# x enters SBUF through DMA transposes from DRAM instead of plain loads, TensorE transposes and PSUM copies (gated mix of a linear-attention block and a one-token mixture, one Trainium2 core)

## The chip, the cores and the metric

The kernel runs on one core of one Trainium2 chip. The metric is the device time of one execution in microseconds (us); a smaller number is better. Times below are either the measured time of whole executions or come from one profiled execution of the kernel.

## The reference, cut to what matters

The input x has 2048 rows (tokens) of 1024 numbers in bf16. Branch A is a linear attention with 32 heads of 32, whose feature map is a pair of softmaxes; branch B passes x through and adds a gated feed-forward result to the one row with the largest logit. A sigmoid gate mixes the two.

```
x = A_x
g = _sigmoid((x * gate_w).sum(-1, keepdims=True))
...
q, k, v = qkv[0], qkv[1], qkv[2]            # qkv from x @ wqkv
pk = jnp.einsum("bhsd,hdf->bhsf", k, w_phi)
phi_k = jnp.concatenate([_softmax(pk, axis=-1), _softmax(-pk, axis=-1)], axis=-1)
kv = jnp.einsum("bhsf,bhsd->bhfd", phi_k, v)
...
r = x @ w_r
idx = jnp.argsort(-r, axis=-1)[:, :C]       # C = 1: one row is chosen
...
return g * a + (1 - g) * b
```

## The kernel before

The work is cut into 16 token tiles of 128 rows (t = 0 to 15), and most stages into 32 units u = 2t + half, a unit being one token tile and 16 heads. Every product with x on TensorE needs x with its columns on the partitions, so the kernel builds `xT`, 128 partitions x 8 blocks x 2048 tokens in bf16, once and keeps it. How `xT` is filled is what the change touches.

**x.** `xload(t)` (L109 to L112) loads one tile of 128 x 1024 from DRAM on the SP queue into a pool of four buffers (`xs`). `xT_tile(t)` (L122 to L134) does eight 128 x 128 transposes on TensorE into a PSUM tile `pT` (L128), copies it into `xT` on VectorE for even t (L130) and on ScalarE for odd t (L132), and then issues the load of tile t + 4.

**Weights.** `wv_sb` (two loads of 1 MB), `wk_raw` (2 MB), later `wo_sb` and `wq_raw` (2 MB each) and 21 chunks of 1 MB of the feed-forward weights also go through the SP queue. `prep_j` (L136 to L147) folds `w_phi` into the k weights, for one block j of eight: eight TensorE transposes of `wk_raw` into PSUM (`pTw`, L139), a VectorE copy `wT` (L141), eight matmuls with the block-diagonal `BDm` into two PSUM tiles (`pW`, L146), and two ScalarE copies into `wkf` (L147). `pTw` and both `pW` share the two buffers of the pool `psB`. The first k unit needs all eight blocks of `wkf`. The q weights go through `prep_j` later.

**Logits and route.** `logits_and_route` (L149 on) multiplies all 16 tiles of `xT` with two columns (L155, 8 matmuls a tile, results in `small_ps`), makes the gates from one column, and finds the row with the largest logit from the other: the column is transposed, moved into one row `r_row` by a small DMA on SP (L168), and searched on VectorE (MAX8, L170; FIND_INDEX8, L172). The index picks a column `xsT` of `xT` (L175), which the feed-forward chunks (L202) then use.

**k units, q units, tail.** A k unit is 8 matmuls for v (L292), 8 for k (L304), a softmax pair over VectorE (mx L243, mn L244, d L251, ssum L263, rs L267), POOL (d L247, phi L269) and ScalarE (pks L235, e L256 and L257), and 8 matmuls that add to `kv_b` (L323). q units (L352 on) and the output projection (L428) follow.

The order of the calls is written by hand in an event list with keys, but the framework's scheduler then decides the order in which instructions stand on each engine; each engine runs its list in order. A wait of an instruction holds up everything behind it on its engine. DMAs use eight completion semaphores in turn, so a DMA on SP waits at least for the one eight places earlier to land.

The calls ahead of the k units are:

```
    for t in range(4):
        xT_tile(t)
    for u in sorted(v_startup, key=lambda u: (u % 2, u)):
        k_v(u)
    for j in range(KB):
        prep_j(wk_raw, wkf, j)
        if j % 2 == 1:
            xT_tile(4 + j // 2)
    for t in range(8, NT):
        xT_tile(t)
```

`v_startup` holds five units. In the program before, TensorE's list starts with transposes of tiles 0 to 2, then v units mixed with tile 3, then `prep_j` blocks mixed with the transposes of later tiles and with the logits of the tiles that are already there; the logits of tiles 13 to 15 and all of the routing stand among the first k units.

Of the kernel before, what the change touches and what calls it, by code (L numbers as in the profile page):

```python
# [8 lines left out]
BF = mybir.dt.bfloat16  # L9
# [8 lines left out]
P = 128  # L18
# [4 lines left out]
NT = S // P  # L23
KB = D // P
# [13 lines left out]
def kernel(  # L38
# [4 lines left out]
    nc = tc.nc  # L43
    x2 = A_x.rearrange("b s d -> (b s) d")
# [8 lines left out]
    psA = ctx.enter_context(tc.tile_pool(name="psA", bufs=2, space=PSUM))  # L53
# [10 lines left out]
    ident = const.tile([P, P], BF, name="ident")  # L64
# [17 lines left out]
    xT = big.tile([P, KB, S], BF, name="xT")  # L82
# [24 lines left out]
    xtiles = {}  # L107

    def xload(t):  # L109
        xt_ = xs.tile([P, D], BF, name="xs_t", tag="xs")  # L110
        nc.sync.dma_start(out=xt_[:], in_=x2[t * P:(t + 1) * P, :])
        xtiles[t] = xt_  # L112

    xload(0)
    nc.sync.dma_start(out=wv_sb[:, :, 0:512], in_=w_v[:, :, 2 * D:2 * D + 512])
    for t in range(1, 4):
        xload(t)
    nc.sync.dma_start(out=wv_sb[:, :, 512:D], in_=w_v[:, :, 2 * D + 512:3 * D])
    wk_raw = raw.tile([P, KB, D], BF, name="wk_raw", tag="wraw")
    nc.sync.dma_start(out=wk_raw[:], in_=w_v[:, :, D:2 * D])  # L120

    def xT_tile(t):  # L122
        if t not in xtiles:
            xload(t)
        xt_ = xtiles.pop(t)
        pT = psA.tile([P, KB, P], BF, name="pT", tag="pA")
        for kb in range(KB):
            nc.tensor.transpose(out=pT[:, kb, :], in_=xt_[:, kb * P:(kb + 1) * P], identity=ident[:])  # L128
        if t % 2 == 0:
            nc.vector.tensor_copy(out=xT[:, :, t * P:(t + 1) * P], in_=pT[:])  # L130
        else:
            nc.scalar.copy(out=xT[:, :, t * P:(t + 1) * P], in_=pT[:])  # L132
        if t + 4 < NT:
            xload(t + 4)  # L134

    def prep_j(w_raw, wf, j):  # L136
        pT = psB.tile([P, KB, P], BF, name="pTw", tag="pB")
# [354 lines left out]
# [10 lines that stand above are left out]
# [43 lines left out]
```

## Time and profile before

| what | value |
|---|---|
| time, median of 2 executions | 356.94 us (355.91 and 357.97) |
| span of the profiled execution | 356.3 us |
| busy: TensorE, VectorE, ScalarE, POOL | 318.7, 258.5, 211.8, 202.8 us |
| L128, transposes of x on TensorE | 128 instructions, 3.8 to 39.4 us |
| L130 / L132, copies of `pT` | 8 of 0.68 us on VectorE / 8 of 1.02 us on ScalarE |
| first k matmul (L304) | 39.4 us |
| last copy of `wkf` (L147) ends | 41.7 us |
| loads of x tiles (`xs_t`) | 16 of 256 KB, 5.5 us to landing (median) |
| DMA bytes in the execution | 43.6 MB |

The span is the time from the first to the last instruction of one execution. "Busy" of TensorE counts modelled ends of pipelined matmuls, so a busy TensorE is not TensorE at its peak. PE is TensorE, PEld its weight loads, DVE VectorE, ACT ScalarE, SP the queue that issues most DMAs.

### The profile page before, as it was taken

How to read it: one execution, taken by the hardware profiler on the slowest of the kernel's cores; microseconds unless marked ns; L12 is line 12 of the kernel's file. 1: busy time of each engine (PE TensorE's matmuls, PEld its weight loads, DVE VectorE, ACT ScalarE, POOL GpSimd, SP SyncE). 2: the span in 40 equal slices, each digit the busy share in tenths (PEclk: the TensorE clock that was granted, in tenths of full speed). 3: DMA queues.
4: the chain of work that ended last, by engine and by line, in shares of the span. 5: the costliest groups of instructions: out<-in, count | busy, mean ns of one | idle time of the engine just before them, and what ended most of it. 6: DMA issues, size and time to landing. Idle time of an engine off the chain costs nothing. (4 is left out here: it accounts for less than half of the span.)

```text
span 356.3 us, 8221 instructions
## 1 busy us (share of the span) xinstructions
PE 318.7 (89%) x3322; PEld 189.1 (53%) x3372; DVE 258.5 (73%) x455; ACT 211.8 (59%) x333; POOL 202.8 (57%) x231
## 2 busy tenths in 40 slices
PE   2998996989989899698989898999999999999982
PEld 1578552445555555354446475555555555556640
DVE  3034288877987975688887989888888888887641
ACT  1456645535556655254554679777777777778630
POOL 1000056467776763577778978687777766665101
PEclk9999999989999999999999999999999999999998
DMA  8997920028823033333336660012221111122111
GB/s 253 375 386 238 324 87 2 0 87 272 261 94 118 2 120 118 120 118 120 120 118 237 233 245 31 31 59 61 61 60 61 60 60 46 59 61 62 47 59 30
DMA packets 33894, 43.60 MB, mean 122 GB/s; under 512 B 2624, under 2 KB 23104, under 8 KB 33856
## 3 DMA queue, kind: packets, MB, share of 16 engines
q1 hardware_dynamic: 32704, 43.00, 35.5%
q8 instruction: 26, 0.43, 0.5%
q10 hardware_dynamic: 1120, 0.07, 0.2%
q14 instruction: 12, 0.10, 0.1%
q0 software_dynamic: 32, 0.00, 0.0%
HBM read 38.87 MB, written 4.20 MB: 121 GB/s over the span
## 5 line engine op out<-in xcount | busy, mean ns | idle before, releaser
L247 POOL TENSOR_TENSOR d<-pks,mx 128x512 bf16<-128x512 bf16 x64 | 67.1, 1049 | 89.1 <-DVE mx L243 82.4
L263 DVE TENSOR_REDUCE ssum<-e 128x32 f32<-128x1024 bf16 x64 | 77.4, 1211 | 33.3 <-ACT e L257 33.2
L256 ACT ACTIVATE e<-d 128x512 bf16<-128x512 bf16 x64 | 40.5, 633 | 61.7 <-POOL d L247 55.4
L269 POOL TENSOR_TENSOR phi<-e,rs 128x1024 bf16<-128x1024 bf16 x32 | 61.2, 1912 | 22.0 <-DVE rs L267 21.0
L304 PE MATMUL pk<-wkf,xT 128*128 128x512 bf16 x242 | 61.7, 385 | 4.6 <-DVE d L251 4.1
L352 PE MATMUL pq<-wqf,xT 128*128 128x512 bf16 x237 | 59.2, 379 | 3.9 <-ACT pks L235 2.0
L292 PE MATMUL pv<-wv_sb,xT 128*128 128x512 bf16 x248 | 61.1, 385 | 0.8 <-issue 0.2
L428 PE MATMUL kv_b<-wo_sb,oT 128*128 128x512 bf16 x247 | 57.1, 379 | 1.5 <-ACT oT L416 1.0
L243 DVE TENSOR_REDUCE mx<-pks 128x16 f32<-128x512 bf16 x64 | 42.4, 662 | 17.2 <-ACT pks L235 13.9
L257 ACT ACTIVATE e<-d 128x512 bf16<-128x512 bf16 x64 | 40.4, 631 | 7.6 <-POOL d L249 7.2
L374 ACT COPY eT<-eT_ps 128x1024 bf16<-128x1024 bf16 x32 | 32.6, 1019 | 17.6 <-PE eT_ps L370 17.6
L244 DVE TENSOR_REDUCE mn<-pks 128x16 f32<-128x512 bf16 x64 | 42.8, 669 | 0.0
L428 PEld LDWEIGHTS <-oT 128*128 128x128 bf16 x256 | 24.8, 98 | 30.2 <-ACT oT L416 1.1
L304 PEld LDWEIGHTS <-xT 128*128 128x128 bf16 x256 | 24.2, 98 | 30.2 <-issue 5.9
L292 PEld LDWEIGHTS <-xT 128*128 128x128 bf16 x256 | 24.1, 99 | 27.3 <-issue 3.1
L352 PEld LDWEIGHTS <-xT 128*128 128x128 bf16 x256 | 24.1, 97 | 27.0 <-issue 2.7
L277 POOL TENSOR_TENSOR e<-e,rho 128x512 bf16<-128x512 bf16 x32 | 33.6, 1051 | 2.5
L249 POOL TENSOR_TENSOR d<-pks,mn 128x512 bf16<-128x512 bf16 x32 | 33.6, 1049 | 1.4
L431 DVE SCALAR_TENSOR_TENSOR o_out<-kv_b,gate,xg 128x512 bf16<-128x512 f32 x32 | 23.8, 744 | 10.6 <-PE kv_b L428 7.9
L141 DVE COPY wT<-pTw 128x1024 bf16<-128x1024 bf16 x16 | 10.9, 683 | 19.7 <-PE pTw L139 19.7
L296 ACT CAST vaug<-pv 128x512 bf16<-128x512 f32 x32 | 18.6, 581 | 8.5 <-PE pv L292 8.4
L235 ACT CAST pks<-pk 128x512 bf16<-128x512 f32 x32 | 18.5, 578 | 5.7 <-PE pk L304 4.7
(94 smaller groups left out, 432.9 us busy)
## 6 DMA issues: line engine op xcount, KB each, us to landing
wch<-in_B_w_gate_dram SPq DMA_DIRECT2D x7, 1024.0 KB, 6.0
wch<-in_B_w_up_dram SPq DMA_DIRECT2D x7, 1024.0 KB, 5.1
wchd<-in_B_w_down_dram SPq DMA_DIRECT2D x7, 1024.0 KB, 5.2
xs_t<-in_A_x_dram SPq DMA_DIRECT2D x16, 256.0 KB, 5.5
xin<-in_A_x_dram SPq DMA_DIRECT2D x16, 256.0 KB, 2.7
out_dram<-o_out SPq DMA_DIRECT2D x32, 128.0 KB, 1.7
wv_sb<-in_A_wqkv_dram SPq DMA_DIRECT2D x2, 1024.0 KB, 5.7
wk_raw<-in_A_wqkv_dram SPq DMA_DIRECT2D x1, 2048.0 KB, 10.1
```

Source lines behind the costliest of these rows:

```text
L243: nc.vector.tensor_reduce(out=mx[:], in_=st["ps"][:], axis=AX.X, op=ALU.max)
L244: nc.vector.tensor_reduce(out=mn[:], in_=st["ps"][:], axis=AX.X, op=ALU.min)
L247: nc.gpsimd.tensor_tensor(out=d1[:], in0=st["ps"][:], in1=_bc(mx[:], [P, HH, DH]), op=ALU.subtract)
L249: nc.gpsimd.tensor_tensor(out=d2[:], in0=st["ps"][:], in1=_bc(mn[:], [P, HH, DH]), op=ALU.subtract)
L256: nc.scalar.activation(out=e[:, :, 0, :], in_=st["d1"][:], func=ACTF.Exp)
L257: nc.scalar.activation(out=e[:, :, 1, :], in_=st["d2"][:], func=ACTF.Exp, scale=-1.0)
L263: nc.vector.tensor_reduce(out=ssum[:].rearrange("p h s -> p (h s)"), in_=e[:].rearrange("p h s f -> p (h s) f"), axis=AX.X, op=ALU.add)
L269: nc.gpsimd.tensor_tensor(out=phi[:].rearrange("p h s f -> p (h s) f"), in0=e[:].rearrange("p h s f -> p (h s) f"), in1=_bc(rs[:].rearrang ...
L292: nc.tensor.matmul(pvf, lhsT=xT[:, kb, t * P:(t + 1) * P], rhs=wv_sb[:, kb, hf * 512:(hf + 1) * 512], start=(kb == 0), stop=(kb == KB - 1))
L304: nc.tensor.matmul(pkf, lhsT=xT[:, kb, t * P:(t + 1) * P], rhs=wkf[:, kb, hf * 512:(hf + 1) * 512], start=(kb == 0), stop=(kb == KB - 1))
L352: nc.tensor.matmul(pqf, lhsT=xT[:, kb, t * P:(t + 1) * P], rhs=wqf[:, kb, hf * 512:(hf + 1) * 512], start=(kb == 0), stop=(kb == KB - 1))
L428: nc.tensor.matmul(kv_b[nh][:], lhsT=oT[:, kb, :], rhs=wo_sb[:, kb, sl], start=(kb == 0), stop=(kb == KB - 1))
```

## The change

`xT_tile(t)` becomes one DMA on the SP queue that reads 128 rows of x from DRAM and writes them transposed into `xT`. The first four loads of x that stood among the weight loads are gone, so `wv_sb` and `wk_raw` are now issued ahead of all of x. The 128 transposes of x on TensorE, the 16 copies out of PSUM, and the 16 plain loads are no longer there; `prep_j`, the logits and everything later are unchanged in the source.

```
-    xload(0)
     nc.sync.dma_start(out=wv_sb[:, :, 0:512], in_=w_v[:, :, 2 * D:2 * D + 512])
-    for t in range(1, 4):
-        xload(t)
     nc.sync.dma_start(out=wv_sb[:, :, 512:D], in_=w_v[:, :, 2 * D + 512:3 * D])
     wk_raw = raw.tile([P, KB, D], BF, name="wk_raw", tag="wraw")
     nc.sync.dma_start(out=wk_raw[:], in_=w_v[:, :, D:2 * D])
 
     def xT_tile(t):
-        if t not in xtiles:
-            xload(t)
-        xt_ = xtiles.pop(t)
-        pT = psA.tile([P, KB, P], BF, name="pT", tag="pA")
-        for kb in range(KB):
-            nc.tensor.transpose(out=pT[:, kb, :], in_=xt_[:, kb * P:(kb + 1) * P], identity=ident[:])
-        if t % 2 == 0:
-            nc.vector.tensor_copy(out=xT[:, :, t * P:(t + 1) * P], in_=pT[:])
-        else:
-            nc.scalar.copy(out=xT[:, :, t * P:(t + 1) * P], in_=pT[:])
-        if t + 4 < NT:
-            xload(t + 4)
+        nc.sync.dma_start_transpose(out=xT[:, :, t * P:(t + 1) * P], in_=x2[t * P:(t + 1) * P, :])
```

The scheduler also moves instructions. In the changed program the lists stand as follows. On SP: `wv_sb` twice, `wk_raw`, the 16 transposes in the order of t, `wo_sb`, `r_row`, two feed-forward chunks, `wq_raw`, and the rest as before. On TensorE: v units of tiles 0 and 1, logits of tiles 0, 1 and part of 2, three more v units, `pTw` of block 0, then the logits of tiles 2 to 15 around the `pW` of block 0, with `pTw` of block 1 between the first and the second logits matmul of tile 15, and only then the rest of blocks 1 to 7; the k matmuls of unit 0 stand between blocks 4 and 6. On VectorE the gate arithmetic, MAX8 and FIND_INDEX8 and the first mx, mn and d of unit 0 stand between the `wT` copies of blocks 1 to 7. Line numbers after the change are 14 lower from `prep_j` on.

## The prediction

> **What bounds the kernel now.** I read the slices of the page first, then the DMA view and the timeline of the first 45 us, where all of x is transposed, then the windows and the groups of VectorE behind it.
>
> From the page, busy tenths and DMA in 40 slices of 8.9 us:
>
> ```profile
> PE   2998996989989899698989898999999999999982
> DVE  3034288877987975688887989888888888887641
> ...
> DMA  8997920028823033333336660012221111122111
> ```
>
> TensorE is full from the second slice on; VectorE is nearly idle in slices 2 to 5 and nearly full afterwards. DMA is full only in the first 45 us. So two stages matter: the front, up to the last block of `wkf`, and the first k units behind it.
>
> The timeline, one block of `prep_j` in the front (start, duration, engine, line):
>
> ```profile
> 22.81 0.61 PE L139 MATMUL pTw<-ident,wk_raw 128*128 128x128 bf16 x8
> ...
> 23.46 0.69 DVE L141 COPY wT<-pTw 128x1024 bf16<-128x1024 bf16 x1 [1.18 <-PE pTw L139]
> ...
> 24.27 0.61 PE L146 MATMUL pW<-BDm,wT 128*128 128x128 bf16 x8
> ...
> 24.69 1.07 ACT L147 CAST wkf<-pW 128x512 bf16<-128x512 f32 x2 [0.53 <-PE pW L146]
> ...
> 25.33 0.61 PE L139 MATMUL pTw<-ident,wk_raw 128*128 128x128 bf16 x8
> ```
>
> The block after starts when the first `pW` copy frees a PSUM buffer: 25.33 - 22.81 = 2.52 us a block, a chain over three engines. The transposes of x run in its gaps. The chain starts at 20.3, because five v units stand first, and ends at 41.7.
>
> Stages by window (columns: length, busy of PE, PEld, DVE, ACT, POOL with instructions, clock, DMA share, GB/s):
>
> ```profile
> 12.50:20.00 7.50, 7.45 (x35) 3.32 (x35) 0.00 (x0) 3.06 (x5) 0.00 (x0) 1.00 1.05 388
> 20.00:39.40 19.40, 17.60 (x324) 15.63 (x323) 8.59 (x14) 12.69 (x20) 0.00 (x0) 1.00 0.90 315
> ...
> 45.00:72.00 27.00, 24.00 (x165) 11.47 (x166) 23.66 (x42) 13.53 (x27) 14.34 (x15) 1.00 0.06 23
> ```
>
> In the first k units (45 to 72) VectorE is busy 23.66 of 27 us and sets the pace; the route's two long searches are in it:
>
> ```profile
> L172 DVE FIND_INDEX8 ix<-mx,r_row 1x8 uint32<-1x2048 bf16 x1 | 2.3, 2273 | 0.0
> L170 DVE MAX8 mx<-r_row 1x8 f32<-1x2048 bf16 x1 | 2.3, 2269 | 0.0
> ```
>
> What a DMA packet costs, from the DMA view of 0 to 45 us (packets, MB, share of 16 engines):
>
> ```profile
> DMA packets 10410, 14.23 MB, mean 316 GB/s; under 512 B 1472, under 2 KB 5568, under 8 KB 10407
> ...
> q1 hardware_dynamic: 9287, 14.11, 89.7%
> q10 hardware_dynamic: 1120, 0.07, 1.7%
> ```
>
> q1: 0.897 x 16 x 45 us / 9287 = 69.5 ns for 1519 B. q10 (the small `BDm` loads): 0.017 x 16 x 45 / 1120 = 10.9 ns for 62 B. A line through both: 8.4 ns a packet plus 0.040 ns a byte.
>
> **What the skill says.** (1) "DMA: Bandwidth & Descriptors", Latency and other measured facts: a DMA transpose moved 261 GB/s with a strided middle dimension, 350 to 400 if contiguous. (2) "VectorE: DVE Perf Modes", The three transpose paths: a 128x128 bf16 transpose takes 1309 ns by DMA. No transpose by DMA is in this trace, so neither is tested; they differ tenfold here. (3) "DMA: Bandwidth & Descriptors", Queues, rings and completion order: a DMA engine takes one queue's descriptors in ring order. The trace agrees: `wk_raw`, issued at 8.0 behind x loads and half of `wv_sb`, landed only at 18.1. (4) "TensorE: Matmul & The Clock Gate", What's actually happening: TensorE runs at half clock until about 3.4 us of steady work. The trace agrees: the first v matmuls at 9.8 take 0.43 us each, from 12.8 on 0.21.
>
> **The change part by part.** r is the time of one 256 KB transpose when they follow one another.
>
> Removed: 128 TensorE transposes (12.0 us), 8 VectorE copies (5.5), 8 ScalarE copies (8.2). I cost them at nothing. From 20 us they fill gaps of the 2.52 us chain; if that chain were faster, their 8 us on TensorE after 20 us would be the most to gain. Ahead of 20 us they take some 4 us before the v units, but there the arrival of `xT` takes over.
>
> Added: 16 transposes behind 4.2 MB of weights, where x had come first. `wk_raw` still waits for the first `BDm` load (issue at 8.0 now); `wv_sb` has drained by then (2.1 MB at 375 GB/s from 1.9 us: 7.5). Issue to first byte 1 us, then 2.1 MB at 375 GB/s, 5.6 us: 14.6. The transposes' reads begin then, and 1.4 us go to the last landing (128 KB of output lands in 1.7, of which 0.35 is transfer). The last tile lands at T = 16 + 16r.
>
> The value of r: a plain x load is 262144 B at 375 GB/s, 0.70 us, the floor. If the transpose reads runs of 256 B, there are 1024 packets, 64 per engine, each 8.4 + 0.040 x 256 = 18.7 ns: 1.2 us. Skill (1) gives 1.0. If writes in pieces of 32 B (16 tokens to one partition) each cost a packet, 8192 / 16 x 9.7 ns = 5.0 us. If blocks run one by one as in skill (2), 8 x 1.309 = 10.5 us. I take 1.5: the read side plus a quarter. T = 40.0.
>
> Moved, the wait that matters: TensorE's list puts the logits of tiles 2 to 15 ahead of blocks 1 to 7. A logits load waits for its tile, and the seven blocks, with the k matmuls of unit 0, are queued behind it. VectorE, ScalarE and POOL wait for these. The five v units run while the transposes land (T - 16 us is enough for their 8.6 us) and hide there. So the front ends at T plus the chain: 6 x 2.52 + 2.9 (last `pTw` start to last `wkf` end, 38.8 to 41.7) = 18.0; VectorE's list now has MAX8 and FIND_INDEX8 between the `wT` copies. A block leaves it 2.52 - 0.69 = 1.83 free, so MAX8 (2.27) adds 0.4, mx + mn + FIND_INDEX8 (0.69 + 0.67 + 2.34 = 3.7) 1.9, d and the register read 0.4: 2.7. Front end: 40.0 + 20.7 = 60.7, against 41.7: **+19.0**.
>
> Given back in the k units: MAX8, FIND_INDEX8 and the gate arithmetic (6.1 us of VectorE) and mx, mn, d of unit 0 (2.1) leave the stage where VectorE sets the pace, 8.2 us; TensorE loses 0.8 us of logits there. At VectorE's 88% share not all counts: **-7**, bounds -4 and -10.
>
> Clock: between T and the end of the front TensorE has 1.23 us of matmuls per 2.52. If its clock halves, each block is up to 0.9 us longer, 6 in all; I take **+1.5**, bounds 0 and 6.
>
> At no cost: `wo_sb` (first read after 200 us) and `wq_raw` (first `wqf` copy at 96.9) come later but hidden; `r_row` queues behind 2.1 MB of `wo_sb`, 5.6 us, and lands near T + 7, ahead of MAX8's place at T + 8. If the queue is slower than that, MAX8 holds `wT` of block 5 one for one. The first chunk is due at c_bc, after the front. Units after these run as before.
>
> Sum against the profiled span: 356.3 + 19.0 - 7 + 1.5 = 369.8. The median of the runs is 0.6 above the span: **370**.
>
> In general, time = 346.4 + 16r.
>
> **The rivals.** *Plain speed, the other side*: the crossbar keeps up with a plain load, r = 0.70, T = 27.2, front +6.2, gives back 10, no clock loss: 356.9 - 3.8 = 353, not slower. For: skill (1)'s 350 to 400 GB/s, and VectorE's fullness. Against: 256 B reads and a strided destination. It decides below r = 0.94, with the full 10 back. *Write side*: 32 B writes bound it, r = 5.0: 426. For: the 8.4 ns a packet costs here whatever its size. Against: skill (1). TensorE then waits most of T = 96 us. *Block by block*: r = 10.5, 514. For: skill (2). Against: that figure holds the fixed cost of one small DMA (1.7 us for 128 KB here), which overlaps when eight are in flight. *No effect*: excluded; the first k unit can't run before `xT` and `wkf` exist.
>
> **How the numbers follow.** Likeliest (r 1.2 to 2.2, 365 to 382): 0.47. Plain speed (r up to 1.2): 0.15. Write side (r 2.2 to 5.2): 0.24. Block by block and beyond: 0.14. The range 358 to 428 leaves out the last and the lower part of the second. About 2% (7.1 us) is what a measurement of this kernel can tell from no change: slower than 364 takes nearly all of the first, and the third and fourth: 0.78; within 2% 0.19; faster 0.03.
>
> **What would show it.** T, as the last landing of a transpose, near 40 us; 24 us from first to last landing; TensorE waiting for `xT` at L141; blocks 1 to 7 of `prep_j` from T on at 2.5 us each; MAX8 inside the front; the span from the end of the front to the end of the kernel some 7 us shorter than 314.6. I would be wrong if the landings are spaced by other than 1.5 us, which multiplies by 16, or if the back part doesn't shorten.

## The result and the profile after

The changed kernel takes **373.43 us** (median of 2 executions, 372.53 to 374.34) against 356.94: a ratio of 1.044, interval 1.032 to 1.057. It is slower. Its profiled execution has a span of 372.7 us against 356.3, 16.4 us more.

The busy tenths and the DMA row of the changed kernel, in slices of 9.3 us:

```profile
PE   0294676999998988999897988999999999999982
...
DVE  2000364588778877578788788998888888887741
...
PEclk9996576999999999999999899999999999999998
DMA  8999934133442333333323675111221221111110
```

Up to slice 7 TensorE is half empty, and its granted clock falls there to 0.5 to 0.7. From slice 8 on the rows look like those of before. The loss lies in the first 65 us.

The group of the added transposes (issue duration in ns as least/median/most, first and last start, then the time to landing, then who waited):

```profile
L120 SPq DMA_TRANSPOSE xT<-in_A_x_dram x16: 1307/1310/5629, 6.1 to 34.1; - x16
...
  PE pv L278: 10.6, 1
...
  PE small_ps L141: 5.4, 6
...
DMA to landing us min/median/max: 3.7/4.0/10.2
```

The two lines that begin with PE say that TensorE waited 10.6 us for the first tile and 5.4 us in all for six later ones. The last transpose starts to issue at 34.1 and lands some 3.7 later. The timeline shows the same tile from TensorE's side, and then the chain of `prep_j` (start, duration, engine, line; in brackets the idle time before it and what ended it):

```profile
33.16 0.37 PE L141 MATMUL small_ps<-wrgT,xT 128*128 128x2 bf16 x8 [1.65 <-DMA xT<-in_A_x_dram]
...
37.85 0.18 PE L141 MATMUL small_ps<-wrgT,xT 128*128 128x2 bf16 x1 [0.86 <-DMA xT<-in_A_x_dram]
...
40.98 1.01 PE L125 MATMUL pTw<-ident,wk_raw 128*128 128x128 bf16 x8
...
42.02 0.69 DVE L127 COPY wT<-pTw 128x1024 bf16<-128x1024 bf16 x1 [0.84 <-PE pTw L125]
...
42.77 1.03 PE L132 MATMUL pW<-BDm,wT 128*128 128x128 bf16 x8 [0.79 <-DVE wT L127]
43.42 1.07 ACT L133 CAST wkf<-pW 128x512 bf16<-128x512 f32 x2 [2.01 <-PE pW L132]
...
44.05 1.01 PE L125 MATMUL pTw<-ident,wk_raw 128*128 128x128 bf16 x8 [0.25 <-ACT wkf L133]
...
48.37 1.49 PE L290 MATMUL pk<-wkf,xT 128*128 128x512 bf16 x3 [0.22 <-issue]
48.79 2.27 DVE L156 MAX8 mx<-r_row 1x8 f32<-1x2048 bf16 x1
...
50.50 1.06 PE L290 MATMUL pk<-wkf,xT 128*128 128x512 bf16 x2
...
52.13 0.69 DVE L127 COPY wT<-pTw 128x1024 bf16<-128x1024 bf16 x1 [1.06 <-PE pTw L125]
...
54.44 2.27 DVE L158 FIND_INDEX8 ix<-mx,r_row 1x8 uint32<-1x2048 bf16 x1
...
57.36 0.62 PE L132 MATMUL pW<-BDm,wT 128*128 128x128 bf16 x8 [2.80 <-DVE wT L127]
...
60.87 1.07 ACT L133 CAST wkf<-pW 128x512 bf16<-128x512 f32 x2 [0.95 <-PE pW L132]
```

The last tile is there at 37.85 (T), and only then do blocks 1 to 7 run. A block of this stage takes 44.05 - 40.98 = 3.07 us where it took 2.52, because the two groups of eight matmuls last 1.01 and 1.03 instead of 0.61. The first search (MAX8) holds nothing: the `wT` after it, at 52.13, waited for TensorE's `pTw`, which stood behind k matmuls of unit 0. The second search (FIND_INDEX8) does hold the next `wT`, so TensorE idles 2.80 before 57.36. The front ends at 60.87 + 1.07 = 61.94.

The windows of the changed kernel: first tile to T, T to the end of the front, and 27 us of k units (columns as in the table of before: length, busy of PE, PEld, DVE, ACT, POOL, clock, DMA share, GB/s):

```profile
16.39:37.85 21.46, 15.96 (x176) 8.95 (x177) 0.69 (x1) 4.01 (x7) 0.00 (x0) 0.84 1.09 180
37.85:61.94 24.09, 16.34 (x137) 12.03 (x140) 13.67 (x24) 9.69 (x20) 1.15 (x2) 0.64 0.55 180
65.00:92.00 27.00, 26.61 (x212) 13.45 (x214) 19.44 (x32) 14.23 (x26) 15.98 (x16) 1.00 0.32 102
```

While the transposes land, the DMA queues move 180 GB/s, about half of the 388 that loads moved before. From T on the clock is 0.64. In the k units VectorE has fallen from 23.66 to 19.44 busy of 27, and TensorE has risen from 24.00 to 26.61.

So: front 61.94 against 41.70, **+20.2**; everything behind it 372.7 - 61.94 = 310.8 against 314.6, **-3.8**; together 16.4.

### The profile page after: what moved, and what is told of

It reads as the page before. It is cut to its first block, busy times and chain, and to the rows that moved or that the text cites. A ratio compares the mean times of both kernels' runs of the same rounds, so it can differ in the third digit from the quotient of the medians.

```text
span 372.7 us, 7953 instructions
## 1 busy us (share of the span) xinstructions
PE 318.3 (85%) x3195; PEld 185.3 (50%) x3244; DVE 253.3 (68%) x447; ACT 204.2 (55%) x325; POOL 202.9 (54%) x231
## 5 line engine op out<-in xcount | busy, mean ns | idle before, releaser
L278 PE MATMUL pv<-wv_sb,xT 128*128 128x512 bf16 x247 | 63.0, 397 | 12.3 <-DMA xT<-in_A_x_dram 10.6
L290 PE MATMUL pk<-wkf,xT 128*128 128x512 bf16 x244 | 62.6, 385 | 4.8 <-DVE d L237 3.3
L338 PE MATMUL pq<-wqf,xT 128*128 128x512 bf16 x237 | 60.3, 384 | 4.0 <-ACT pks L221 2.0
L278 PEld LDWEIGHTS <-xT 128*128 128x128 bf16 x256 | 24.8, 101 | 41.7 <-DMA xT<-in_A_x_dram 10.7
L290 PEld LDWEIGHTS <-xT 128*128 128x128 bf16 x256 | 24.4, 99 | 31.0 <-issue 7.4
L338 PEld LDWEIGHTS <-xT 128*128 128x128 bf16 x256 | 24.3, 98 | 27.5 <-issue 3.7
L417 DVE SCALAR_TENSOR_TENSOR o_out<-kv_b,gate,xg 128x512 bf16<-128x512 f32 x32 | 23.8, 745 | 10.6 <-PE kv_b L414 7.9
L237 DVE TENSOR_TENSOR d<-pk,mn 128x512 bf16<-128x512 f32 x32 | 21.0, 655 | 0.3
```

Of the source, the lines that this page charges most:

```text
L278: nc.tensor.matmul(pvf, lhsT=xT[:, kb, t * P:(t + 1) * P], rhs=wv_sb[:, kb, hf * 512:(hf + 1) * 512], start=(kb == 0), stop=(kb == KB - 1))
L290: nc.tensor.matmul(pkf, lhsT=xT[:, kb, t * P:(t + 1) * P], rhs=wkf[:, kb, hf * 512:(hf + 1) * 512], start=(kb == 0), stop=(kb == KB - 1))
L338: nc.tensor.matmul(pqf, lhsT=xT[:, kb, t * P:(t + 1) * P], rhs=wqf[:, kb, hf * 512:(hf + 1) * 512], start=(kb == 0), stop=(kb == KB - 1))
```

## The experiments

Each was compared with the kernel before on the same chip; the median of that kernel was 356.8 to 357.0 us each time. The diffs are against the changed kernel, unless the text says otherwise. "Front" is the end of the last `wkf` copy.

### The wait taken away: logits behind the blocks

The logits weights `wrgT` now also read (times zero) the last piece of `wkf`, so no logits matmul can stand ahead of a block. The transposes stay as they are.

```
-        nc.vector.tensor_copy(out=wrgT[:], in_=wrgT_ps)
+        nc.vector.scalar_tensor_tensor(out=wrgT[:], in0=wkf[:, KB - 1, D - 16:D], scalar=0.0, in1=wrgT_ps,
+                                       op0=ALU.mult, op1=ALU.add)
```

> The changed kernel, with the two-column weights of the logits made to depend on the last block of wkf (0 times 16 of its columns is added), so that all logits stand behind the eight blocks of prep_j on TensorE; the DMAs are unchanged. My theory (the blocks queue behind logits that wait for the last tile): the transposes still land at 38, but the blocks run from about 28 on, the front ends at 48 to 52, the routing falls back into the k units, and the time is 361 to 367. Rival (late x as such costs the time, whatever the list): the time stays at 371 to 375.

Measured: 366.29 us, ratio 1.026 (1.021 to 1.031). Part of its timeline, the starts of five of the eight blocks and one `pW` group:

```profile
29.27 0.61 PE L125 MATMUL pTw<-ident,wk_raw 128*128 128x128 bf16 x8 [0.45 <-ACT wkf L133]
...
30.66 1.03 PE L132 MATMUL pW<-BDm,wT 128*128 128x128 bf16 x8 [0.79 <-DVE wT L127]
...
31.94 1.01 PE L125 MATMUL pTw<-ident,wk_raw 128*128 128x128 bf16 x8 [0.25 <-ACT wkf L133]
...
35.02 1.01 PE L125 MATMUL pTw<-ident,wk_raw 128*128 128x128 bf16 x8 [0.25 <-ACT wkf L133]
...
41.68 0.61 PE L125 MATMUL pTw<-ident,wk_raw 128*128 128x128 bf16 x8
...
44.14 0.61 PE L125 MATMUL pTw<-ident,wk_raw 128*128 128x128 bf16 x8 [0.45 <-ACT wkf L133]
```

A block takes 3.08 us (35.02 - 31.94) while its groups last 1.01 and 1.03, and 2.46 later, with groups of 0.61. The blocks no longer wait for T: in the profiled execution, the fastest of four at 363.76, the front ends at 49.5, 12.4 earlier. A transpose holds SP as long as before (1.307 us least), and the last is issued at 32.7, where it was 34.1. The part behind is 312.6, since the routing is in the k units again. By the medians, 7.1 of the 16.5 us were the place of the logits, not the transposes themselves. Most of what the front still loses (7.8 us) is there before its chain begins: the first block starts at 26.80, 6.5 later than before, because the five v units wait for the first tile behind the weights.

### x first

The SP order of before with transposes for loads: tile 0, half of `wv_sb`, tiles 1 to 3, the other half, `wk_raw`, the rest. The logits keep their place.

```
+    xT_tile(0)
     nc.sync.dma_start(out=wv_sb[:, :, 0:512], in_=w_v[:, :, 2 * D:2 * D + 512])
+    for t in range(1, 4):
+        xT_tile(t)
     nc.sync.dma_start(out=wv_sb[:, :, 512:D], in_=w_v[:, :, 2 * D + 512:3 * D])
```

> The changed kernel with the SP order of the kernel before: tile 0, half of wv, tiles 1 to 3, the other half, wk_raw, then the other tiles; same bytes, same transposes, and the scheduler then puts the logits of tiles 4 to 15 one by one between the blocks. My theory: the last tile still lands at 37 to 40, but only the blocks 6 and 7 stand behind it, the front ends at 46 to 49 and the time is 357 to 363. Rival (the rate of the transposes alone costs it): 371 to 375, as the last landing does not move.

Measured: 363.36 us, ratio 1.019 (1.011 to 1.026). The last transpose still issues only at 35.5, but the scheduler now mixes the blocks with the logits, and the front ends at 49.35; front and time lie 0.4 us above what was expected. The date of the last tile hardly moved and yet 10.1 of the 16.5 us are gone, so that date alone did not cost them. The order of the weights changed too, so this isn't the blocks' place alone. Its first line on the SP queue is of use below:

```profile
0.89 1.37 SPq L116 DMA_TRANSPOSE xT<-in_A_x_dram  x1
```

With nothing ahead of it in the queue, one transpose occupies SP for 1.37 us.

### Plain loads in pieces of 256 B

The transposition is left out: the same tile is written to the same place by a plain load whose rows are cut in pieces of 256 B, so `xT` holds x untransposed.

```
-        nc.sync.dma_start_transpose(out=xT[:, :, t * P:(t + 1) * P], in_=x2[t * P:(t + 1) * P, :])
+        nc.sync.dma_start(out=xT[:, :, t * P:(t + 1) * P], in_=x2[t * P:(t + 1) * P, :].rearrange("p (kb c) -> p kb c", c=P))
```

> The changed kernel with a plain load into the same places of xT in place of each transpose: the transposition is left out, the runs stay 256 bytes long on both sides. If the 256-byte packets set the rate, tiles land 1.2 us apart (my line through the packets of before, 18.7 ns) or up to 1.4 (23 ns, what the transposes show), the last at 34 to 37, time 368 to 373. If the crossbar sets it, plain tiles land 0.7 us apart, the last near 26 and the time is 360 to 363.

Measured: 367.71 us, ratio 1.030 (1.024 to 1.036). The stretch from 18 to 26 us, first of the changed kernel, then of this one:

```profile
18.00:26.00 8.00, 7.95 (x49) 3.67 (x49) 0.00 (x0) 1.76 (x3) 0.00 (x0) 1.00 1.08 199
```

```profile
18.00:26.00 8.00, 8.00 (x51) 3.63 (x50) 0.00 (x0) 1.76 (x3) 0.00 (x0) 1.00 1.37 218
```

218 GB/s is 262144 / 218000 = 1.20 us a tile: the prediction's price for the read side (1024 packets, 18.7 ns each) was right to a few per cent, and the DMA share of 1.37 shows more work in the engines than the transposes put there (1.08). Pieces of 256 B, loaded plainly, therefore explain 1.2 us, not 1.43. The total, 0.3 us below the expected 368 to 373, says less: here the scheduler also set the logits of tiles 13 to 15 among the blocks, so the front (50.8) isn't one of T alone.

### Four large transposes in place of sixteen

```
-        nc.sync.dma_start_transpose(out=xT[:, :, t * P:(t + 1) * P], in_=x2[t * P:(t + 1) * P, :])
+        if t % 4 == 0:
+            nc.sync.dma_start_transpose(out=xT[:, :, t * P:(t + 4) * P], in_=x2[t * P:(t + 4) * P, :])
```

> The changed kernel with 4 transposes of 512 rows in place of 16 of 128. If the packets set the rate (my theory), 4 MB still take about 22 us from first to last and the time is 371 to 376. If the issue on SP (1.31 us an instruction) or a fixed cost of each instruction sets it, they take under 17 us and the time is 364 to 368.

Measured: 371.22 us, ratio 1.039 (1.034 to 1.045). The group of its transposes, and its landings:

```profile
L121 SPq DMA_TRANSPOSE xT<-in_A_x_dram x4: 3919/4268/10957, 6.1 to 25.5; - x4
...
DMA to landing us min/median/max: 6.2/6.2/13.2
```

3.92 us for 512 rows is 0.98 us per 128 rows against 1.31. The same bytes and the same transposition, in fewer instructions, take SP 25% less time: the stretch from 18 to 26 us moves 245 GB/s for 199. The last tile lands near 25.5 + 6.2 = 31.7, 6 us before the changed kernel's. From 19.3, when the first four tiles are there, the other twelve take 12.4 us, 1.04 us each; this is the faster spacing that was expected if the issue or a fixed cost of each instruction sets it. The time gains only 2.2 and so lies in the band that was expected if packets set the rate; the landings decide, as the time has another cause. The first four tiles come together, so the first v matmul starts at 19.3 (16.4 before); the v units and then the logits follow without a wait for `xT`, and the front still ends at 58.6. Here TensorE's own list, no longer the landing, sets the start of the blocks.

### A contiguous destination

`xT` is laid out as 128 x 16 x 8 x 128, so that one transpose writes one unbroken run of each partition. The row that the feed-forward uses is read from a wrong place in this layout, with the same instructions.

```
-    xT = big.tile([P, KB, S], BF, name="xT")
+    xT = big.tile([P, NT, KB, P], BF, name="xT")
...
-        nc.sync.dma_start_transpose(out=xT[:, :, t * P:(t + 1) * P], in_=x2[t * P:(t + 1) * P, :])
+        nc.sync.dma_start_transpose(out=xT[:, t], in_=x2[t * P:(t + 1) * P, :])
```

> The changed kernel with xT laid out so that each transpose writes 2 KB in one piece in every partition; the chosen row's column is then read from another place, so the feed-forward runs on another row's numbers. If the issue on SP sets the rate (1.31 us an instruction), tiles stay 1.35 us apart and the time stays at 371 to 375. If the strided destination sets it, tiles land about 0.7 to 1.0 us apart, the last near 30 to 33, and the time is 364 to 368.

Measured: 372.86 us, ratio 1.045 (1.042 to 1.048).

```profile
L120 SPq DMA_TRANSPOSE xT<-in_A_x_dram x16: 1307/1308/5338, 6.1 to 33.6; - x16
...
DMA to landing us min/median/max: 3.6/3.9/9.9
```

The time and the issue hardly move, and the stretch from 18 to 26 us moves 193 GB/s for 199. With transposes of 128 rows the stride of the destination isn't what limits them.

### The clock kept up

Four matmuls whose result nobody reads are added behind each block from 1 on; all transposes are called first.

```
+    def keep_busy():
+        pD = psA.tile([P, 512], F32, name="pD", tag="pA")
+        for _ in range(4):
+            nc.tensor.matmul(pD[:], lhsT=xT[:, 0, S - P:S], rhs=wv_sb[:, 0, 0:512], start=True, stop=True)
...
         prep_j(wk_raw, wkf, j)
+        if j > 0:
+            keep_busy()
```

> The changed kernel with four added 512-column matmuls a block (7 blocks, into an unused buffer, nobody reads them) that read tile 15, so that TensorE stays busy while blocks 1 to 7 of prep_j run; these blocks still stand behind the last landing, but the last logits and all of the routing now stand behind the blocks. If the half clock is what makes a block 3.08 us after the change (my theory), a block takes 2.5 to 2.6, the front ends 18 to 19 us after the last landing in place of 24.1, and the part after it is 312 to 315 us, as the routing is back in it: 369 to 372. If the chain's waits make it, blocks stay at 3.08 and the time is 374 to 377.

Measured: 371.91 us, ratio 1.042 (1.039 to 1.045). Its timeline:

```profile
44.33 0.61 PE L130 MATMUL pTw<-ident,wk_raw 128*128 128x128 bf16 x8
...
45.72 0.62 PE L137 MATMUL pW<-BDm,wT 128*128 128x128 bf16 x8
...
46.79 0.61 PE L130 MATMUL pTw<-ident,wk_raw 128*128 128x128 bf16 x8
```

With more work on TensorE the block is shorter: 46.79 - 44.33 = 2.46 us, not 3.07, and the groups are back at 0.61. The front ends 57.08 - 37.33 = 19.75 after T, where it was 24.1, although the first of its blocks, still at half clock and with added matmuls between its groups, took 4.13. Not all of the 4.3 us gained in the front are the clock: the scheduler put the searches back into the k units here, and the part behind the front is 2.4 us longer for it.

### The fold of the k weights first

If the wait is for x, the work that needs no x can go ahead of it. SP's order becomes `wk_raw`, half of `wv_sb`, tiles 0 to 2, the other half, tiles 3 to 15; the five v units are spread over the blocks and use the other PSUM pool; the logits stand behind as in the first experiment. Of the edit, the order of the blocks and v units is shown.

```
     for j in range(KB):
         prep_j(wk_raw, wkf, j)
-        if j % 2 == 1:
-            xT_tile(4 + j // 2)
+        if 2 <= j < 7:
+            k_v(vs[j - 2])
```

> A version meant to use the transposes: SP order wk_raw, half of wv, tiles 0 to 2, the rest of wv, tiles 3 to 15; the blocks of prep_j stand first on TensorE with the five early v units between them (in the other PSUM pool), and the logits stand behind the blocks. My theory (only the place of the waits makes the change slow): the blocks run from 9 or 10 us on at 2.5 to 2.7 us each, the front ends at 31 to 34, and the time is 346 to 350, faster than before. Rival (transposes in flight slow the weights or starve the first units): 353 or more.

Measured: **353.17 us** (352.04 to 353.81), ratio 0.989 (0.986 to 0.992): faster than both kernels, against the kernel before by 1.1%, a small gain that the interval sets apart from none. The front ends at 33.3, as expected; slow weights or starved first units, the rival's cause, would have shown there. But the time lies above the expected band, at the edge of the rival's (353 or more), because the part behind the front takes 318.6, 4.0 more than before. The stage from the end of the front to the first `wqf` copy, of this kernel and then of the kernel before:

```profile
33.32:92.90 59.58, 54.21 (x574) 28.97 (x573) 45.82 (x75) 26.31 (x51) 32.67 (x33) 0.94 0.64 197
```

```profile
41.70:96.90 55.20, 50.31 (x494) 26.95 (x502) 43.81 (x74) 26.36 (x51) 32.46 (x33) 0.97 0.39 131
```

The stage is 4.4 us longer and TensorE is busy 3.9 us longer in it. Part is seen in the timeline: all 128 logits matmuls stand here, at 43.67 in one row of 3.55 us, where 24 of them took 0.78 before, and the v unit behind them runs at half clock (six matmuls in 2.56 us). The rest I didn't take apart.

### The same order with TensorE transposes

Is that gain one of order alone? Two kernels give the kernel *before* the same order of weights, blocks and v units, with plain loads and TensorE transposes. The first still had four load buffers; of its edit too, only the order of the calls is shown:

```
 (against the kernel before)
     for j in range(KB):
+        if j >= 1:
+            xT_tile(j - 1)
         prep_j(wk_raw, wkf, j)
+        if 3 <= j:
+            k_v(vs[j - 3])
```

> The same order of loads, blocks, v units and late logits, but in the kernel before, with plain loads of x and transposes on TensorE. If the order alone makes the gain, it is as fast as the version with DMA transposes, 346 to 350. If freeing TensorE of the transposes is worth something once nothing waits for them (my theory), its front ends 3 to 5 us later, at 35 to 38, and the time is 350 to 354.

Measured: 362.26 us, ratio 1.016 (1.012 to 1.019); a miss. Its blocks end at 35.75, but the loads of the later tiles wait for a free buffer and stand on SP behind 2 MB of `wo_sb`, the last five also behind 2 MB of `wq_raw` (issued at 33.34, landed at 43.1), and the k matmuls stand behind the transposes of these tiles: the first starts at 48.46. So a second control has nine buffers and a later `wo_sb`, and all its x loads are issued before `wq_raw` (the line of the buffers is shown):

```
 (against the first control)
-    xs = kscope.enter_context(tc.tile_pool(name="xs", bufs=4))
+    xs = kscope.enter_context(tc.tile_pool(name="xs", bufs=9))
```

> The control for the wk-first order, with the cause of the miss of the control before taken away: x by plain loads and TensorE transposes, nine load buffers instead of four, wo_sb issued later, so that no x load stands behind 2 MB of weights. If the gain of the wk-first kernel is one of order alone and TensorE has room for the transposes, the first k matmul comes by 36 us and the time is 350 to 354. If the DMA transposes are needed for it, since the 128 transposes (12 us of TensorE) and 16 copies now stand in a front that TensorE fills, the first k matmul comes at 38 us or later and the time is 355 to 360.

Measured: 358.07 us, ratio 1.004 (1.002 to 1.005). Its timeline between the last block and the first k unit:

```profile
36.65 1.08 PE L129 MATMUL pT<-ident,xs_t 128*128 128x128 bf16 x16
...
42.22 3.62 PE L309 MATMUL pk<-wkf,xT 128*128 128x512 bf16 x15
```

No x load is late any more and the last block's copy ends at 35.2, and still the first k unit starts at 42.22: from 35 to 42 TensorE works, with hardly a gap, through v matmuls and the transposes of the remaining tiles. In the kernel with DMA transposes and this order the first k matmul came at 30.86. So this order of weights and blocks gains nothing with transposes on TensorE, as the scheduler laid them out here (358.07), and gains with DMA transposes (353.17). The two kernels differ also in load buffers and in the place of `wo_sb`, and a list with the first k unit ahead of the late transposes wasn't tried.

## Why the prediction was right, and where its terms were off

The mechanism was as predicted: the logits hold the blocks until T, then the seven blocks run, and less is given back in the k units. The span came to 372.7 where the sum gave 369.8; the total is nearer than its terms, because one of them was off the other way. Term by term:

- **T**: 40.0 predicted, 37.85 measured, -2.2. The first tile was there at 16.4 (17.5 predicted). From there the tiles came 21.46 / 15 = 1.43 us apart, for r = 1.5. `wk_raw` didn't wait for `BDm`: it was issued at 2.4, not at 8.0; the step was wrong, and without effect, since the same bytes were ahead of the transposes.
- **What r is made of**: the step "the read side plus a quarter" hit the number for a reason that the runs refute; that r came out near was luck. Plain loads in pieces of 256 B do cost 1.20 us a tile. But large transposes need less, 0.98 us of SP for 128 rows, so that price is no floor for them. The transposes of 128 rows take SP 1.31 us each (1.37 with an empty queue), most land a near constant 3.7 to 4.1 after their issue starts, the destination's layout is of no matter, and fewer and larger ones are faster. They follow SP's issue, with one delay of some 2 us near 30 us that I did not explain; the run with the logits behind the blocks doesn't have it. Whether SP is held by making the transpose's descriptors or by something behind it stays open.
- **The chain behind T**: 20.7 plus 1.5 for the clock predicted, 24.1 measured, +1.9. The search lengthened its block as priced (58.43 - 53.95 = 4.48, 1.96 over 2.52; predicted 1.9). Two terms of the sum, 0.8 together, cost nothing: MAX8 held no `wT`, and neither did d and the register read. The clock term was mis-sized. Three blocks at 3.07 and the last one (3.5 for 2.9) cost 0.55 to 0.6 each at half clock. The block with MAX8 took 51.35 - 47.13 = 4.22, 1.70 over, because five k matmuls of unit 0 stand between its groups, at half clock too; in the run with added matmuls, a block with k matmuls between its groups took 51.72 - 49.25 = 2.47 at full clock. Together this is 4.0 where I took 1.5, inside the bounds of 0 to 6: 2.5 more for the clock and 0.8 less for the other terms nearly make up the +1.9.

  The run with added matmuls shows the clock as cause. The Trainium skill, "TensorE: Matmul & The Clock Gate", What's actually happening, has the clock fall after an idle window of about 3.4 us. No idle stretch of that length was needed here: in the first experiment the clock fell inside the chain, between 29.27 (0.61 a group) and 30.66 (1.03), where TensorE was never idle for more than 0.79 us at a stretch.
- **The give-back**: -7 predicted, -3.8 measured, +3.2. VectorE did lose the work (43.81 to 36.55 busy from the end of the front to the first `wqf` copy), but that stage shrank only from 55.20 to 52.16. The other 0.8 us came later. The step that failed is "at VectorE's 88% share not all counts": it asked only how much of VectorE's relief counts, and TensorE was the next limit. Before, TensorE idled 27.00 - 24.00 = 3.0 us between 45 and 72; afterwards it is busy 26.61 of 27, so in these units little was left to gain.

  The step also took the clock as whole again at the end of the front. It was not: TensorE's v matmuls start 0.43 us apart until 64.87 (second view below), so the v unit across the end of the front takes 64.87 - 61.51 = 3.36 us, where the v unit at this place took 42.99 - 41.27 = 1.72 before. Of the 2.93 us behind the front at half clock about half, 1.5, is lost (an estimate from these starts). The share of each cause in the 3.2 is read from these figures; no run tested it.

The v unit at the end of the front, of the kernel before and then of the changed kernel:

```profile
41.27 1.89 PE L292 MATMUL pv<-wv_sb,xT 128*128 128x512 bf16 x8
42.99 2.54 PE L304 MATMUL pk<-wkf,xT 128*128 128x512 bf16 x11
```

```profile
61.51 0.59 PE L278 MATMUL pv<-wv_sb,xT 128*128 128x512 bf16 x1 [0.24 <-ACT wkf L133]
...
62.31 2.77 PE L278 MATMUL pv<-wv_sb,xT 128*128 128x512 bf16 x6 [0.22 <-issue]
...
64.87 2.09 PE L290 MATMUL pk<-wkf,xT 128*128 128x512 bf16 x8
```

-2.2 + 1.9 + 3.2 = +2.9, the whole difference between 369.8 and 372.7. The plain-speed rival fell with 218 GB/s for plain 256 B pieces and 1.31 us of issue; the write side with 1.43 us instead of 5.0, and with the packets themselves; block by block with a spacing seven times shorter than 10.5. The packets under 512 B, first before and then after the change:

```profile
DMA packets 33894, 43.60 MB, mean 122 GB/s; under 512 B 2624, under 2 KB 23104, under 8 KB 33856
```

```profile
DMA packets 48485, 43.58 MB, mean 117 GB/s; under 512 B 19264, under 2 KB 39744, under 8 KB 48448
```

These are 16640 more, 1040 a transpose, or some 252 B each; with a packet for each piece of 32 B there would be 8192 a transpose.

The 1309 ns that the Trainium skill gives for a DMA transpose of a 128x128 block ("VectorE: DVE Perf Modes", The three transpose paths) is, here, what one instruction of eight such blocks holds SP (1307 to 1310 ns). No run transposes one block alone.

## What to carry to other kernels

When a load is moved or slowed, look first for the instructions that wait for it on an in-order engine and at what is queued behind them: here 7 of 16 us came from small matmuls standing ahead of work that needed no x. Taking the transposes off a busy TensorE gained here only once the order of the rest was made to fit the order in which data now came. And when a stage's slowest engine is relieved, look at the idle time of the next one before promising more: here TensorE went from 24.00 to 26.61 busy of 27 us. Last, price a lower clock for as long as it lasts, also behind the stage in which it fell.

## What was not expected of the hardware

One DMA transpose of 128 x 1024 bf16 takes the SP queue 1.31 us and lands 3.7 us after its issue starts; one of 512 x 1024 takes 3.9 us and lands after 6.2. Plain loads of 1 MB on that queue took 0.46 and 0.57 us when it was free. Between 18 and 26 us sixteen small transposes moved 199 GB/s, four large ones 245, and plain loads in pieces of 256 B 218: large transposes were faster than such plain loads. And unused matmuls made a chain of small matmuls faster, 2.46 us a block for 3.07.
